# A decode step's last head pair: V between two parts of W_o, all its values as columns, W_o on whole partitions

## The chip, the cores and the metric

One core of a Trainium2 chip runs the kernel. The time is device time in microseconds (us) of one execution. A profiled execution also has a span, from its first to its last instruction, and the profile's times count from the span's start. TensorE does the matrix products, VectorE (DVE) and ScalarE (ACT) the element-wise work, GpSimd (POOL) some set-up, and SyncE (SP) issues nearly all the transfers from HBM, in one queue, over 16 DMA engines.

## The reference

Two sequences (B = 2) decode one token each. The first block is attention over a cache with 32 heads of 128, of 8192 positions each; the second a gated feed-forward block.

```
h  = x + A(layernorm(x))
h2 = h + F(layernorm(h))

A(x):  q = x @ wq                                  # 512 -> 32 heads x 128
       p = softmax(q . k_cache * 128**-0.5)        # per sequence and head, over 8192 positions
       return concat(p . v_cache) @ wo             # 4096 -> 512
F(x):  g = x @ W_gate;  u = x @ W_up               # 512 -> 1376
       return (max(g, 0) * u) @ W_down             # 1376 -> 512
```

All inputs are bfloat16. Each cache has 2 x 32 x 8192 x 128 elements, 134 MB; with the weights 281 MB have to come in from HBM.

## The kernel before

**Steps.** The 64 heads (32 of each sequence) are worked through in steps of four heads, 0 to 14 (14 is LASTQ, called Q); the last four heads are two pairs, p0 and p1. A step takes one tile of K and one of V, 8 MB each (4 MB for a pair): 128 partitions with 256 columns of 128 elements, so each partition holds 256 positions of one head (128 for a pair). Three buffers of this size, bufs[0] to bufs[2], go round. Everything is in an order written out by hand (manual_schedule), so that each engine and SP's queue take their instructions in program order.

**Scores.** products (L373) multiplies K by the broadcast q on VectorE, scores (L391, L393) sums each column's 128 elements by halving, in place. NPE columns of a step are done by TensorE instead (scores_pe: transposes, a copy on ScalarE per 8 columns, products with q). For p0 and p1, 40 columns are summed by ScalarE (act_sums, L379). The softmax takes the largest score: within a partition group for a four-head step (largest_of_own, no TensorE), through a product into PSUM for a pair (largest, L404), followed by exponentials on ScalarE (L431).

**Values.** values (L444) takes the shares of four columns as the stationary operand and 512 elements of V as the moving one, one product per four columns, into a PSUM row block; diagonals (L456) then picks the useful blocks out and turns them into columns. values_cols (L487) does the other way round: V's 128 x 128 block is stationary and two columns of shares move, and the result stands as a column at once. For p1 the kernel before does the first 64 of 128 columns by wide products (values_mixed, L468, then a copy on ScalarE and diagonals_mixed, L479) and the rest by values_cols into the same sums.

**Output projection.** W_o lies in the upper half of bufs[0]. The first 28 heads come in sets (SETS) with consecutive rows of W_o in one partition, so that a partition's piece is 16, 8 or 4 KB; the heads' results then have to be laid out anew to match (spread on VectorE, L499, lay_rows on TensorE and VectorE, L510 and L511), and attend_set (L517) multiplies. The last four heads are loaded by head, in rows of 1 KB, and attend (L524) takes them as they are:

```
for r0, r1 in ((0, P - 4), (P - 4, P)):            # L578: 124 rows, then 4
    nc.sync.dma_start(out=wo[r0:r1, HM * D:(HM + 2) * D]..., in_=_dram(A_wo, ...))
```

**The end.** hc (L640) adds the input. A normalisation and the feed-forward block follow: g_ps (gate), u_ps (up), d_ps (down, L690), whose weights are loaded last, gate and up into the upper half of bufs[2], W_down into bufs[1]. Only products with few columns are left there.

**Transfers.** A transfer's issue waits on SP until its buffer is free, and everything behind it in the queue waits as well. Each transfer signals one of eight semaphores in rotation, so an issue can also wait for the transfer eight places ahead of it. K of step i + 2 is issued when values of step i are done (it takes V's buffer), V of step i + 1 when scores of step i are done. The order at the end is: K of p0 and p1, V of p0, all of W_o (six transfers), V of p1 in four pieces (into the lower half of bufs[2], which values(Q) reads), gate, up in two parts, W_down in seven pieces.

Of the kernel before, what the change touches and what calls it, by code (L numbers as in the profile page):

```python
# [7 lines left out]
ACT = mybir.ActivationFunctionType  # L8
# [10 lines left out]
def _dram(t, offset, dims):  # L19
    return bass.AP(tensor=t.tensor, offset=t.offset + offset, ap=[list(d) for d in dims])  # L20
# [3 lines left out]
def kernel(  # L24
# [13 lines left out]
    nc = tc.nc  # L38
    P = nc.NUM_PARTITIONS
    B, Sq, D = A_x.shape  # L40
    _, Hkv, Sk, Dh = A_k_cache.shape
    Hq = A_wq.shape[1] // Dh
# [5 lines left out]
    f32 = mybir.dt.float32  # L48


    NH = 4
    NQ = Hq // NH
    LASTQ = B * NQ - 2
# [3 lines left out]
    VG = 4  # L57


    NPE = 32  # L60
    NPE_AT = {**{i: 24 for i in (1, 2)}, LASTQ: 24, LASTQ + 1: 0, LASTQ + 2: 0}
    NACT = 0
    NACT_AT = {LASTQ + 1: 40, LASTQ + 2: 40}
    NEXT = 16
    WIDE = 16
    QZ = 32


    SETS = [(0, 16, 0), (16, 8, 16), (24, 4, 24)]
    HM = 28  # L70
    SROWS = [n for _, n, _ in SETS]


# [87 lines left out]
    def load_tile(cache, s, dst, pieces=1):  # L161
        h = NH * s.g + (0 if s.quad else 2 * s.k)
        n = s.nt * Dh
        w = n // pieces
        for k in range(pieces):
            nc.sync.dma_start(
                out=dst[:, k * w:(k + 1) * w], in_=_dram(cache, (s.b * Hkv + h) * Sk * Dh + k * w, [[n, P], [1, w]]),
            )
# [19 lines left out]
    with tc.manual_schedule():  # L188
# [97 lines left out]
        o_ps = {}  # L286
# [96 lines left out]
        def scores(s):  # L383

            scol = scols[s.i]
            width = Dh
            while width > 8:
                half = width // 2
                lo = _free(s.kt, s.na * Dh, [[Dh, s.nv - s.na], [1, half]])
                hi = _free(s.kt, s.na * Dh + half, [[Dh, s.nv - s.na], [1, half]])  # L390
                nc.vector.tensor_tensor(out=lo, in0=lo, in1=hi, op=ALU.add)  # L391
                width = half
            nc.vector.tensor_reduce(  # L393
                out=scol[:, s.na:s.nv], in_=_free(s.kt, s.na * Dh, [[Dh, s.nv - s.na], [1, 8]]), axis=AXIS.X, op=ALU.add,
            )
            pms[s.i] = small.tile([P, 1], f32, tag="pm", name="pm", bufs=2)
            nc.vector.tensor_reduce(out=pms[s.i], in_=scol, axis=AXIS.X, op=ALU.max)  # L397
# [3 lines left out]
        def largest(s):  # L401

            mx[s.i] = ps.tile([P, P], f32, tag="mx", name="mx_ps")
            nc.tensor.matmul(out=mx[s.i], lhsT=_free(pms[s.i], 0, [[0, P]]), rhs=nscale, start=True, stop=True)  # L404
# [18 lines left out]
        def exponentials(s):  # L423
            scol = scols[s.i]
            nm = small.tile([P, NH], f32, tag="nm", bufs=2)
            nc.vector.tensor_reduce(
                out=nm[:, 0:s.nh], in_=mx[s.i].rearrange("p (j q) -> p j q", j=s.nh), axis=AXIS.X, op=ALU.min,
            )
            for j in range(s.nh):
                r = s.rows(j)  # L430
                nc.scalar.activation(  # L431
                    out=s.pg[r, :, j, :], in_=scol[r, :].rearrange("p (u t) -> p u t", t=VG), func=ACT.Exp, scale=SCALE,
                    bias=nm[r, j:j + 1], accum_out=s.zc[r, j:j + 1],
                )
# [24 lines left out]
                    start=(t == 0), stop=(t == VG - 1),  # L459
                )  # L460

        def values_mixed(s, u0, u1):

            r = slice(32 * (s.g % 4), 32 * (s.g % 4) + s.nh * VG)
            if u0 == 0:
                pv_ps[s.i] = ps2.tile([P, VG * Dh], f32, tag="o", name="pv_ps")
            for u in range(u0, u1):
                nc.tensor.matmul(  # L468
                    out=pv_ps[s.i][r, :], lhsT=s.pg[:, u].rearrange("p j t -> p (j t)"),
                    rhs=s.vt[:, u * VG * Dh:(u + 1) * VG * Dh], start=(u == 0), stop=(u == WIDE - 1),  # L470
                )
            if u1 == WIDE:
                nc.scalar.activation(out=pv[r, :], in_=pv_ps[s.i][r, :], func=ACT.Copy)

        def diagonals_mixed(s):
            h0 = NH * (s.g % 4)
            o_ps[s.i] = ps2.tile([P, 8], f32, tag="o", name="o_ps")
            for t in range(VG):
                nc.tensor.matmul(  # L479
                    out=o_ps[s.i][:, 0:2], lhsT=pv[:, t * Dh:(t + 1) * Dh],  # L480
                    rhs=pick[:, t].rearrange("p k j -> p (k j)")[:, h0:h0 + 2], start=(t == 0), stop=False,
                )

        def values_cols(s, t0, t1):

            for t in range(t0, t1):
                nc.tensor.matmul(  # L487
                    out=o_ps[s.i][:, 0:2], lhsT=s.vt[:, t * Dh:(t + 1) * Dh],
                    rhs=s.pg[:, t // VG, :, t % VG], start=False, stop=(t == s.nt - 1),
                )  # L490

        att_ps = ps.tile([P, KC, B], f32, tag="acc")
# [1 line left out]
        def spread(k, b):  # L494

            h0, n, _ = SETS[k]
            nq = Dh // n
            sp = qrep[:, B * k + b, :]
            nc.vector.tensor_tensor(  # L499
                out=_free(sp, 0, [[nq, n], [1, nq]]), in0=_free(ocol, h0 * B + b, [[B, n], [0, nq]]),  # L500
                in1=_free(quot[n], 0, [[0, n], [1, nq]]), op=ALU.mult,
            )
            return sp

        def lay_rows(k, sps):

            r = SROWS[k]
            or_ps = ps.tile([P, B, r], f32, tag="mx")
            for b in range(B):
                nc.tensor.matmul(out=or_ps[:, b, :], lhsT=sps[b], rhs=rest[r], start=True, stop=True)  # L510
            nc.vector.tensor_copy(orow[k], or_ps.rearrange("p b c -> p c b"))  # L511

        def attend_set(k, r0=0, r1=None):
            for c0 in range(r0, SROWS[k] if r1 is None else r1):
                for c in range(KC):
                    at = (SETS[k][2] + c0) * D + c * P
                    nc.tensor.matmul(  # L517
                        out=att_ps[:, c, :], lhsT=wo[:, at:at + P], rhs=orow[k][:, c0, :],
                        start=(k == 0 and c0 == 0 and c == 0), stop=False, skip_group_check=True,
                    )  # L520

        def attend(h):
            for c in range(KC):
                nc.tensor.matmul(  # L524
                    out=att_ps[:, c, :], lhsT=wo[:, h * D + c * P:h * D + (c + 1) * P], rhs=ocol[:, h, :],
                    start=False, stop=(h == Hq - 1), skip_group_check=True,
                )
# [43 lines left out]
        place_own(s)  # L571
        products(p0, 0, p0.na)
        own_sums(Q)
        for k, (h0, n, at) in enumerate(SETS):
            nc.sync.dma_start(
                out=wo[:, at * D:(at + n) * D], in_=_dram(A_wo, h0 * Dh * D, [[n * D, P], [1, n * D]]),
            )
        for r0, r1 in ((0, P - 4), (P - 4, P)):  # L578
            nc.sync.dma_start(
                out=wo[r0:r1, HM * D:(HM + 2) * D].rearrange("p (h n) -> p h n", n=D),  # L580
                in_=_dram(A_wo, (HM * Dh + r0) * D, [[D, r1 - r0], [Dh * D, 2], [1, D]]),
            )
        nc.sync.dma_start(
            out=wo[:, (HM + 2) * D:Hq * D].rearrange("p (h n) -> p h n", n=D),
            in_=_dram(A_wo, (HM + 2) * Dh * D, [[D, P], [Dh * D, 2], [1, D]]),
        )
        products(p0, p0.na)

        act_sums(p0)
        values(s, 0, s.nt // VG)  # L590
        load_tile(A_v_cache, p1, p1.vt, pieces=4)
        scores(p0)
        largest(p0)
        products(p1, 0, p1.na)
        exponentials(p0)
        act_sums(p1)
        products(p1, p1.na)
        for w, src, c, n in ((0, B_W_gate, 0, 4), (1, B_W_up, 0, 2), (1, B_W_up, 2, 2)):
            nc.sync.dma_start(
                out=wgu[:, w, c:c + n], in_=_dram(src, c * P * F, [[F, P], [P * F, n], [1, F]]),  # L600
            )
# [9 lines left out]
        nc.vector.reciprocal(out=rzs[Q], in_=z2_ps)  # L611
        values(p0, 0, p0.nt // VG)
        scores(p1)
        attend_set(0, 0, 10)
        diagonals(Q)
        largest(p1)
        attend_set(0, 10)
        normalise(Q)
        sps = [spread(1, b) for b in range(B)]
        exponentials(p1)  # L620
        lay_rows(1, sps)
        sps = [spread(2, b) for b in range(B)]
        attend_set(1)
        lay_rows(2, sps)
        values_mixed(p1, 0, WIDE)
        attend_set(2)
        diagonals_mixed(p1)
        values_cols(p1, VG * WIDE, 3 * p1.nt // 4)
        for h in range(HM, HM + 2):
            attend(h)  # L630
        sums(Q + 2)
        shares(Q + 2)
        values_cols(p1, 3 * p1.nt // 4, p1.nt)
        normalise(Q + 2)
        for h in range(HM + 2, Hq):
            attend(h)


# [93 lines left out]
```

## Time and profile before

| | |
|---|---|
| time, median of 3 runs | 665.35 us (664.29 to 665.5) |
| the profiled execution: its own time, its span | 664.98 us, 663.2 us |
| busy: PE, PEld, DVE, ACT | 54%, 24%, 83%, 20% of the span |
| from HBM | 281.09 MB, 424 GB/s over the span |
| mean granted TensorE clock | 0.773 |
| V of p1: issued, four pieces of 1 MB | 630.08 us and later; 14.0 us to landing (median) |
| W_o, first 16 heads | issued 605.50 us, 25.0 us to landing |
| hc starts; span ends | 654.52 us; 663.2 us |

PE is the matrix products and PEld the loads of their stationary operand. Lnnn is a line of the kernel. Rows of the timeline and of the chain of waits begin with a start and a length in us. The chain follows the work that ended last back through what released it. The windows give, for a stretch of time, the busy time of each engine with its number of instructions in brackets, the granted TensorE clock, the busy share of the DMA engines and the GB/s that they moved.

### The profile page before, as it was taken

How to read it: one execution, taken by the hardware profiler on the slowest of the kernel's cores; microseconds unless marked ns; L12 is line 12 of the kernel's file. 1: busy time of each engine (PE TensorE's matmuls, PEld its weight loads, DVE VectorE, ACT ScalarE, POOL GpSimd, SP SyncE). 2: the span in 40 equal slices, each digit the busy share in tenths (PEclk: the TensorE clock that was granted, in tenths of full speed). 3: DMA queues.
4: the chain of work that ended last, by engine and by line, in shares of the span. 5: the costliest groups of instructions: out<-in, count | busy, mean ns of one | idle time of the engine just before them, and what ended most of it. 6: DMA issues, size and time to landing. Idle time of an engine off the chain costs nothing.

```text
span 663.2 us, 5113 instructions
## 1 busy us (share of the span) xinstructions
PE 357.5 (54%) x2105; PEld 161.1 (24%) x2105; DVE 551.1 (83%) x245; ACT 131.6 (20%) x372; POOL 5.3 (1%) x32
## 2 busy tenths in 40 slices
PE   3530924719184572918358191835719277273787
PEld 1210311304032230403114040311304133021345
DVE  1399697979969797996969799696988979999971
ACT  1130030301103030210303011030300205102760
POOL 3000000000000000000000000000000000000000
PEclk9875876959688695968769596876959779595986
DMA  9999999999999999999999999999999999999995
GB/s 380 443 440 443 443 424 411 435 439 432 443 436 435 415 440 431 432 439 439 432 427 439 428 423 443 432 443 427 432 431 428 435 435 432 427 422 431 417 366 226
DMA packets 8562, 281.40 MB, mean 424 GB/s; under 512 B 858, under 2 KB 2012, under 8 KB 3420
## 3 DMA queue, kind: packets, MB, share of 16 engines
q1 hardware_dynamic: 8536, 281.09, 98.7%
q8 instruction: 16, 0.26, 0.2%
q14 instruction: 6, 0.05, 0.0%
q10 hardware_dynamic: 4, 0.00, 0.0%
HBM read 281.09 MB, written 0.00 MB: 424 GB/s over the span
## 4 chain that ended last, share of the span: by engine, by line
DVE 44%; DMA 33%; PE 19%; ACT 3%; issue 1%; DVEq 0%; ACTq 0%
DMA tile<-in_A_k_cache_dram 31%; DVE tile L373 20%; DVE tile L391 19%; PE pv_ps L444 14%; DVE scol L393 2%; DMA tile<-in_A_wq_dram 2%; ACT tile L379 2%; PE q_ps L253 1%; PE pv_ps L468 1%; DVE pgq L418 1%; ACT ecol L413 1%; DVE pm L397 1%; DVE qrep L393 0%; DVE pm L408 0%; PE o_ps L487 0%
## 5 line engine op out<-in xcount | busy, mean ns | idle before, releaser
L444 PE MATMUL pv_ps<-tile,pgq 128*16 128x512 bf16 x960 | 238.9, 416 | 199.5 <-DVE pgq L418 187.1
L373 DVE TENSOR_TENSOR tile<-tile,qrep 128x28672 bf16<-128x28672 bf16 (+3 forms) x16 | 228.1, 14258 | 55.5 <-DMA tile<-in_A_k_cache_dram 55.5
L391 DVE TENSOR_TENSOR tile<-tile 128x14336 bf16<-128x14336 bf16 (+5 forms) x68 | 233.2, 3429 | 2.3
L444 PEld LDWEIGHTS <-pgq 128*16 128x16 bf16 x960 | 91.6, 97 | 341.2 <-DVE pgq L418 197.4
L350 ACT ACTIVATE tile<-t_ps 128x1024 bf16<-128x1024 bf16 x57 | 56.7, 1022 | 18.4 <-PE t_ps L349 17.5
L449 ACT ACTIVATE pv<-pv_ps 16x512 f32<-16x512 f32 (+1 forms) x16 | 9.4, 588 | 243.3 <-PE pv_ps L444 243.3
L340 PE MATMUL row_ps<-tile,qz 128*32 128x512 bf16 (+1 forms) x114 | 34.8, 387 | 18.6 <-ACT tile L350 18.3
L413 ACT ACTIVATE ecol<-scol,nmax 128x256 bf16<-128x256 f32 x14 | 7.1, 507 | 188.1 <-DVE nmax L412 188.1
L349 PE MATMUL t_ps<-ident,tile 128*128 128x128 bf16 x456 | 34.0, 225 | 5.4 <-DMA tile<-in_A_k_cache_dram 5.4
L349 PEld LDWEIGHTS <-tile 128*128 128x128 bf16 x456 | 26.9, 101 | 22.2 <-issue 16.6
L393 DVE TENSOR_REDUCE scol<-tile 128x224 f32<-128x1792 bf16 (+1 forms) x14 | 28.4, 2029 | 0.5
L308 PE MATMUL z_ps<-zc,ones 128*128 128x16 f32 (+1 forms) x8 | 2.4, 373 | 43.6 <-DVE zc L299 43.6
L379 ACT ACTIVATE tile<-tile 128x128 bf16<-128x128 bf16 x80 | 23.4, 294 | 3.5 <-DVE tile L373 3.5
L418 DVE TENSOR_TENSOR pgq<-ecol,ownb 128x1024 bf16<-128x1024 bf16 x15 | 10.4, 692 | 10.3 <-ACT ecol L413 10.3
L373 DVE TENSOR_TENSOR tile<-tile,qpair 128x5120 bf16<-128x5120 bf16 (+1 forms) x4 | 17.7, 4416 | 0.0
L340 PEld LDWEIGHTS <-qz 128*32 128x32 bf16 (+1 forms) x114 | 9.4, 94 | 28.7 <-issue 22.4
L379 ACT ACTIVATION_READ_ACCUMULATOR tile<-tile 128x1 f32 x80 | 15.0, 187 | 0.0
L256 DVE CAST tile<-q_ps 2x512 bf16<-2x512 f32 x8 | 5.4, 679 | 10.3 <-PE q_ps L253 10.3
L253 PE MATMUL q_ps<-tile,xn 128*2 128x512 bf16 x32 | 9.3, 452 | 8.6 <-DMA tile<-in_A_wq_dram 8.6
L365 ACT ACTIVATE scol<-sc_ps 32x32 f32<-32x32 f32 (+1 forms) x56 | 12.2, 217 | 7.8 <-PE sc_ps L360 7.3
L308 PEld LDWEIGHTS z_ps<-zc,ones 128*128 128x128 f32 x8 | 2.0, 312 | 43.9 <-DVE zc L299 29.0
L360 PE MATMUL sc_ps<-ident_f,tile 32*128 32x32 f32 (+1 forms) x60 | 6.5, 226 | 11.0 <-ACT tile L357 11.0
(127 smaller groups left out, 132.6 us busy)
## 6 DMA issues: line engine op xcount, KB each, us to landing
tile<-in_A_k_cache_dram SPq DMA_DIRECT2D x2, 4096.0 KB, 23.2
tile<-in_A_wq_dram SPq DMA_DIRECT2D x1, 4096.0 KB, 12.3
tile<-in_A_v_cache_dram SPq DMA_DIRECT2D x1, 4096.0 KB, 20.5
tile<-in_A_v_cache_dram SPq DMA_DIRECT2D x4, 1024.0 KB, 14.0
tile<-in_A_wo_dram SPq DMA_DIRECT2D x1, 2048.0 KB, 25.0
tile<-in_B_W_gate_dram SPq DMA_DIRECT2D x1, 1376.0 KB, 16.8
tile<-in_B_W_up_dram SPq DMA_DIRECT2D x2, 688.0 KB
tile<-in_A_wo_dram SPq DMA_DIRECT2D x1, 1024.0 KB, 27.4
```

What stands on the lines that cost most here:

```text
L253: nc.tensor.matmul(out=q_ps, lhsT=xn[:, c, :], rhs=wq_sb[:, c, n0:n0 + 4 * Dh], start=(c == 0), stop=(c == KC - 1),)
L340: nc.tensor.matmul(out=row_ps, lhsT=z, rhs=s.kt[:, (nv + c0 + k) * Dh:(nv + c0 + k + 4) * Dh], start=(u == 0), stop=(u == U - 1),)
L349: nc.tensor.transpose(t_ps[:, k, :], s.kt[:, t * Dh:(t + 1) * Dh], ident)
L350: nc.scalar.activation(out=s.kt[:, (nv + c0) * Dh:(nv + c0 + TPC) * Dh], in_=t_ps.rearrange("p t s -> p (t s)"), func=ACT.Copy,)
L365: nc.scalar.activation(out=scols[s.i][r, nv:s.nt].rearrange("p (u t) -> p t u", t=4), in_=sc_ps[r, :, :, j], func=ACT.Copy,)
L373: nc.vector.tensor_tensor(out=kv, in0=kv, in1=_free(s.qr, 0, [[0, n], [1, Dh]]), op=ALU.mult)
L379: nc.scalar.activation(out=kv, in_=kv, func=ACT.Copy, accum_out=scols[s.i][:, t:t + 1])
L391: nc.vector.tensor_tensor(out=lo, in0=lo, in1=hi, op=ALU.add)
L393: nc.vector.tensor_reduce(out=scol[:, s.na:s.nv], in_=_free(s.kt, s.na * Dh, [[Dh, s.nv - s.na], [1, 8]]), axis=AXIS.X, op=ALU.add,)
L413: nc.scalar.activation(out=ecol, in_=scols[s.i], func=ACT.Exp, scale=SCALE, bias=nmax, accum_out=zs[:, s.b, s.g:s.g + 1],)
L418: nc.vector.tensor_tensor(out=s.pg, in0=_free(ecol, 0, [[VG, s.nt // VG], [0, NH], [1, VG]]), in1=_free(ownb, 0, [[0, s.nt // VG], [VG, NH ...
L444: nc.tensor.matmul(out=pv_ps[s.i][r, :], lhsT=s.pg[:, u].rearrange("p j t -> p (j t)"), rhs=s.vt[:, u * VG * Dh:(u + 1) * VG * Dh], start= ...
```

## The change

Steps 3 to 6 give 24 columns to TensorE instead of 32, as steps 1 and 2 did already. W_o is cut into sets of 16, 8, 4 and 2 heads and one piece with the last two, each on all 128 partitions. On SP's queue V of the last pair comes after the first set, and the rest of W_o after V. The gate is loaded in two parts. All 128 columns of the last pair's V are taken by values_cols; values_mixed and diagonals_mixed are gone. On TensorE the first set is attended whole ahead of the last pair's maximum, the maximum is ahead of diagonals(Q), and the other sets and the last heads are attended after all values are done.

```diff
-    NPE_AT = {**{i: 24 for i in (1, 2)}, LASTQ: 24, LASTQ + 1: 0, LASTQ + 2: 0}
+    NPE_AT = {**{i: 24 for i in range(1, 7)}, LASTQ: 24, LASTQ + 1: 0, LASTQ + 2: 0}
-    WIDE = 16
-    SETS = [(0, 16, 0), (16, 8, 16), (24, 4, 24)]
-    HM = 28
+    SETS = [(0, 16, 0), (16, 8, 16), (24, 4, 24), (28, 2, 28)]
+    HM = 30
...
-        def values_mixed(s, u0, u1):
...
-        def diagonals_mixed(s):
...
         def values_cols(s, t0, t1):
+            if t0 == 0:
+                o_ps[s.i] = ps2.tile([P, 8], f32, tag="o", name="o_ps")
             for t in range(t0, t1):
                 nc.tensor.matmul(
                     out=o_ps[s.i][:, 0:2], lhsT=s.vt[:, t * Dh:(t + 1) * Dh],
-                    rhs=s.pg[:, t // VG, :, t % VG], start=False, stop=(t == s.nt - 1),
+                    rhs=s.pg[:, t // VG, :, t % VG], start=(t == 0), stop=(t == s.nt - 1),
                 )
...
-        for k, (h0, n, at) in enumerate(SETS):
+        def load_set(k):
+            h0, n, at = SETS[k]
             nc.sync.dma_start(
                 out=wo[:, at * D:(at + n) * D], in_=_dram(A_wo, h0 * Dh * D, [[n * D, P], [1, n * D]]),
             )
-        for r0, r1 in ((0, P - 4), (P - 4, P)):
-            nc.sync.dma_start(
-                out=wo[r0:r1, HM * D:(HM + 2) * D].rearrange("p (h n) -> p h n", n=D),
-                in_=_dram(A_wo, (HM * Dh + r0) * D, [[D, r1 - r0], [Dh * D, 2], [1, D]]),
-            )
-        nc.sync.dma_start(
-            out=wo[:, (HM + 2) * D:Hq * D].rearrange("p (h n) -> p h n", n=D),
-            in_=_dram(A_wo, (HM + 2) * Dh * D, [[D, P], [Dh * D, 2], [1, D]]),
-        )
+        load_set(0)
         products(p0, p0.na)
 
         act_sums(p0)
         values(s, 0, s.nt // VG)
         load_tile(A_v_cache, p1, p1.vt, pieces=4)
+        for k in range(1, len(SETS)):
+            load_set(k)
+        nc.sync.dma_start(
+            out=wo[:, HM * D:Hq * D].rearrange("p (h n) -> p h n", n=D),
+            in_=_dram(A_wo, HM * Dh * D, [[D, P], [Dh * D, Hq - HM], [1, D]]),
+        )
...
-        for w, src, c, n in ((0, B_W_gate, 0, 4), (1, B_W_up, 0, 2), (1, B_W_up, 2, 2)):
+        for w, src, c, n in ((0, B_W_gate, 0, 2), (0, B_W_gate, 2, 2), (1, B_W_up, 0, 2), (1, B_W_up, 2, 2)):
...
         values(p0, 0, p0.nt // VG)
         scores(p1)
-        attend_set(0, 0, 10)
+        attend_set(0)
+        largest(p1)
         diagonals(Q)
-        largest(p1)
-        attend_set(0, 10)
+        exponentials(p1)
         normalise(Q)
-        sps = [spread(1, b) for b in range(B)]
-        exponentials(p1)
-        lay_rows(1, sps)
-        sps = [spread(2, b) for b in range(B)]
-        attend_set(1)
-        lay_rows(2, sps)
-        values_mixed(p1, 0, WIDE)
-        attend_set(2)
-        diagonals_mixed(p1)
-        values_cols(p1, VG * WIDE, 3 * p1.nt // 4)
-        for h in range(HM, HM + 2):
-            attend(h)
+        sps = [[spread(k, b) for b in range(B)] for k in range(1, len(SETS))]
+        half = p1.nt // 2
+        values_cols(p1, 0, half)
+        for k in range(1, len(SETS)):
+            lay_rows(k, sps[k - 1])
         sums(Q + 2)
         shares(Q + 2)
-        values_cols(p1, 3 * p1.nt // 4, p1.nt)
+        values_cols(p1, half, p1.nt)
         normalise(Q + 2)
-        for h in range(HM + 2, Hq):
+        for k in range(1, len(SETS)):
+            attend_set(k)
+        for h in range(HM, Hq):
             attend(h)
```

More of the change, by code (lines that the diff above doesn't have):

```diff
@@ L460, in diagonals @@
                 )
-        def values_mixed(s, u0, u1):
[L464 to L470, printed above, removed]
-                )
-            if u1 == WIDE:
-                nc.scalar.activation(out=pv[r, :], in_=pv_ps[s.i][r, :], func=ACT.Copy)
-        def diagonals_mixed(s):
[L476 to L481, printed above, removed]
-                )
         def values_cols(s, t0, t1):
+            if t0 == 0:
+                o_ps[s.i] = ps2.tile([P, 8], f32, tag="o", name="o_ps")
             for t in range(t0, t1):
@@ L577 @@
             )
-        for r0, r1 in ((0, P - 4), (P - 4, P)):
-            nc.sync.dma_start(
-                out=wo[r0:r1, HM * D:(HM + 2) * D].rearrange("p (h n) -> p h n", n=D),
-                in_=_dram(A_wo, (HM * Dh + r0) * D, [[D, r1 - r0], [Dh * D, 2], [1, D]]),
-            )
-        nc.sync.dma_start(
-            out=wo[:, (HM + 2) * D:Hq * D].rearrange("p (h n) -> p h n", n=D),
-            in_=_dram(A_wo, (HM + 2) * Dh * D, [[D, P], [Dh * D, 2], [1, D]]),
-        )
+        load_set(0)
         products(p0, p0.na)
```

## The prediction

> **What bounds the kernel now.** I read the page first for who is busy: the transfers. Section 2 has the core's DMA engines at nine tenths in every slice but the last, while the bytes per second fall only in the last two slices.
>
> ```profile
> DMA  9999999999999999999999999999999999999995
> GB/s 380 443 440 443 443 424 411 435 439 432 443 436 435 415 440 431 432 439 439 432 427 439 428 423 443 432 443 427 432 431 428 435 435 432 427 422 431 417 366 226
> ```
>
> The trace's record of completions (one per DMA engine and transfer) says it more sharply: on the engine that finishes first, each 8 MB tile lands 19.35 us after the one before it, for all 30 tiles in the steps. Nothing that computes costs time there as long as each load is issued before the one ahead of it has drained. The end of the span is different, so I then read the chain of waits from its end (start, length, what):
>
> ```profile
> 639.82 0.60 ACT pv L449
> 640.46 1.06 PE o_ps L456 x8
> 641.52 0.32 PE mx_ps L404 x2
> ...
> 643.90 5.89 PE pv_ps L468 x16
> 649.82 0.04 issue
> 649.87 0.60 ACT pv L473
> 650.47 0.04 issue
> 650.51 1.05 PE o_ps L479 x8
> 651.57 0.82 PE o_ps L487 x32
> ```
>
> From about 640 us TensorE's order of work sets the end, and its largest piece is the last pair's 16 wide products (L468, 5.89 us). The same 32 column products that follow take 0.82 us. Last, the windows of 2 us around the transfers of W_o (columns: busy times, granted clock, DMA share, GB/s):
>
> ```profile
> 630.00:632.00 2.00, 2.00 (x7) 0.66 (x6) 2.00 (x1) 2.00 (x15) 0.00 (x0) 0.62 1.01 371
> 632.00:634.00 2.00, 2.00 (x11) 0.80 (x10) 2.00 (x3) 2.00 (x15) 0.00 (x0) 1.00 1.02 287
> 634.00:636.00 2.00, 2.00 (x11) 0.78 (x9) 1.97 (x2) 2.00 (x15) 0.00 (x0) 1.00 1.08 287
> 636.00:638.00 2.00, 2.00 (x45) 1.28 (x43) 1.97 (x2) 2.00 (x15) 0.00 (x0) 1.00 0.99 313
> 638.00:640.00 2.00, 0.14 (x6) 0.05 (x3) 1.93 (x3) 1.98 (x14) 0.00 (x0) 1.00 1.06 436
> ```
>
> The engines are fully busy, yet move 287 GB/s instead of some 425. This is when W_o's 1 KB rows (L579, L583) pass; by the packet records they take 66 ns each, and 8 KB packets beside them over 400 ns instead of 312. The 124-row piece completes on four engines only (634.9, 635.6, 637.5 and 638.1 us). Two of the four were among the latest already. The lag between first and last engine was 3.5 us when the first 16 heads landed (627.0 to 630.5) and is 5.1 us when the last quarter of V does (643.5 to 648.65). The last piece of W_down lands at 659.09, on the lagging engine; its first use would be at about 660.2. So behind TensorE's chain the transfers are only 1 us away from being the bound.
>
> **Part 1, steps 3 to 6 with 24 columns by TensorE instead of 32.** VectorE gets 8 columns more. The chain shows both sizes: the product is 15.63 us with 232 columns and 15.10 with 224, the four additions 7.90, 4.03, 2.10, 1.14 against 7.63, 3.90, 2.04, 1.10, the sum 2.10 against 2.03; together 1.1 us a step. TensorE and ScalarE lose 8 transposes, two wide products and a 1.02 us copy (L350). V's next load is issued when the scores are done; in these steps that is 4.35 us before the first engine drains, and becomes 3.2. K's load, behind the values, has 4.1 to 5.6 and becomes 3.0 or more. The smallest margin in the trace, at the V load of step 13, is 2.3 us, and no engine went dry there. Cost: nothing. The cover is that margin; without it each of four steps would pay up to 1.1 us.
>
> **Part 2, the order on SP's queue.** V of the last pair goes behind the first 16 heads of W_o. Its four issues wait for values(Q) in quarters (32 of the 64 products from 607.68 us, so until about 617), and SP holds the rest of W_o, the gate, up and down loads behind them. At 617 us V of the first pair (lands at 625.6) and 2 MB of W_o are still queued, and the first engine runs dry at 627.0, so the wait is hidden with some 10 us of cover. Later issues wait for a completion eight transfers back; in the new order each finds at least 4 us of work queued. Before, the last two W_down pieces went out only at 652.2 and 653.9, after gate and the first half of up. Now the gate comes in two parts and they wait for its second part and the first half of up, due near 649 and 651.
>
> W_o's pieces become 8, 4 and 2 KB rows and one piece of 1 KB rows (256 packets instead of 512), all on 16 engines. On the lagging engine, with measured differences between successive landings: 630.5 + four quarters of V at 2.5 + the 1 MB and 0.5 MB sets at 2.47 and 1.26 + 8 packets of 2 KB at 0.65 (between 46 ns for 1 KB and 111 ns for 2.75 KB) + 16 of 1 KB at 0.8 to 1.1 + gate 3.46 + up 3.44 + down 0.33 + 1.88 + four at 0.34 = 656.3 us. To it comes what I can't see: the slowdown beside the 1 KB rows, nothing to 1.2 us (half of the 2.1 to 2.6 us that the windows above lost), and an instruction fetch of 1 us that may hit this engine or not. I take 0.6 in all, since the 1 KB pieces of W_down at the end run at 46 to 49 ns and slow nobody: 656.9 us, 2.2 earlier than now. Bounds 656.3 and 658.5.
>
> **Part 3, TensorE's chain.** The first set's 64 products are done by 638.9 (40 took 1.15 us from 636.99), inside the wait for the maximum, which VectorE delivers at 640.40. Taken ahead of the diagonals, the largest (0.49 us) is done at 640.9 instead of 641.85; the exponentials follow the reduction on VectorE and four ScalarE pieces (642.05 to 643.42 now), so the shares stand at 642.3 us. The diagonals (1.06) fit in between; behind them queue normalise and six spreads (VectorE, 0.48 a pair), done near 643.7, under the columns. Columns: 64 at 0.87 us for 32 is 1.74, to 644.1; their V landed by 635.5, where before the second quarter came at 643.63 and was itself what the wide products waited for. Three lay_rows at 0.40 each (two products 0.14, copy 0.18, two handovers): 645.3. Sums 0.43, columns 1.74, normalise 0.2: 647.7. Then 64 products of attend that used to lie partly under other work, 0.99 for 32: 649.7. hc starts at about 649.7 instead of 654.52, 4.8 us earlier. What goes is 5.89 + 0.60 + 1.05 with three handovers; what comes is 1.74 of columns, one lay_rows and the attends.
>
> That rests on the row of 0.82 to 0.99 us for 32 column products with their weight loads (0.98 us for 32), at half as at full granted clock. [...]
>
> **The sum.** hc to the end takes 8.7 us now (654.52 to 663.2), so the chain alone would end at 658.4. But gate lands near 650, up near 653.5, and W_down at 656.9, on which d_ps then waits: four products and the handover 0.25, and from y to the end 2.85 (660.35 to 663.2): 660.0 us, 3.2 less than now. The transfers take the bound from TensorE and keep 1.6 of its 4.8 us. The profiled execution took 664.98 us for its span of 663.2, so 661.8; against the median of 665.35, which is 0.4 higher, 662.2.
>
> **The rivals.**
>
> *The lag stays.* If the slow windows come from reading W_o's rows at all, the last piece still lands at 659.1 and the end is 659.1 + 3.1 = 662.2, 1.0 us gained: 664.3. For it: half of the 1 KB packets are still there. Against: the lag grew on just those engines that took the 124 rows. Chance 0.10.
>
> *TensorE's chain stays the bound.* If I overrate the down loads, 658.4 to 659, gain 4.2 to 4.8: 660.8. It needs the lagging engine to speed up to 655.5, below the sum with no penalty. Chance 0.06.
>
> *Slower: the loads of steps 3 to 6 run dry.* VectorE's 1.1 us is paid four times as soon as a load needs more than 3.2 us from issue to first byte: 4.4 us lost against 3.2 gained, 1.2 slower, 666.5. Against: the margin of 2.3 us at step 13 without a gap. For: VectorE is the busiest engine (83%), idle only 3.5 us before each product. Chance 0.07, with everything else that ends slower.
>
> [...] Chance 0.05.
>
> **How the numbers follow.** The forecast has the remaining 0.72, between 661.4 (656.3 as the last landing) and 663.7 (658.5), of which none is within 0.2% of the median. That share, 1.3 us, is about what a measurement of this kernel can tell; the three runs shown differ by 1.2. The range takes in the chain as the bound and the lag that stays, 660.9 to 664.4. Faster: 0.72 + 0.06 and some of the lag, 0.81. Within 0.2%: most of the lag and of the chain not freed, 0.11. Slower: 0.08.
>
> **What would show it.** Right: in the chain of waits, L468 and L479 gone, hc at about 650, and d_ps waiting for W_down; windows from 630 us at 400 GB/s or more; V's quarters issued before 620 us; first-engine landings still 19.35 us apart in steps 3 to 6. Wrong: a DMA share under 0.9 between 130 and 310 us, an idle TensorE ahead of the columns for V, or d_ps starting with no wait.

## The result, and the profile after

The changed kernel takes 661.55 us in the median of six runs (661.18 to 662.02), the kernel before 665.25 in six (664.29 to 666.09): ratio 0.9945, 95% interval [0.9932, 0.9958], 3.7 us faster. The forecast was 662.2. The profiled execution took 661.18 us with a span of 659.4, against a forecast span of 660.0.

The two rows of the page for the 40 slices of the span, as they stood before the prediction:

```profile
DMA  9999999999999999999999999999999999999997
GB/s 382 445 442 445 402 430 437 445 446 434 402 441 434 441 438 417 437 429 438 441 430 425 433 426 441 441 422 441 418 442 434 430 433 433 430 421 430 423 410 273
```

Nothing dips in the slices of steps 3 to 6, and the last two slices hold 410 and 273 GB/s where they held 366 and 226. The windows where W_o passes (the same columns as before):

```profile
630.00:632.00 2.00, 2.00 (x7) 0.54 (x5) 2.00 (x1) 2.00 (x15) 0.00 (x0) 0.50 1.01 422
632.00:634.00 2.00, 2.00 (x6) 0.61 (x5) 2.00 (x3) 2.00 (x15) 0.00 (x0) 0.50 1.00 418
634.00:636.00 2.00, 2.00 (x9) 0.75 (x8) 1.98 (x1) 2.00 (x15) 0.00 (x0) 0.86 1.04 434
636.00:638.00 2.00, 2.00 (x11) 0.78 (x9) 1.95 (x2) 2.00 (x16) 0.00 (x0) 1.00 0.99 414
638.00:640.00 2.00, 2.00 (x62) 1.56 (x61) 1.93 (x3) 1.98 (x14) 0.00 (x0) 1.00 1.01 418
```

The stretch of 287 GB/s is gone. The end of the chain of waits:

```profile
638.03 12.80 DMA tile<-in_B_W_up_dram
650.83 0.02 issue
650.85 0.02 SPq L583
650.86 0.03 issue
650.89 5.32 DMA tile<-in_B_W_down_dram
656.21 0.05 issue
656.26 0.28 PE d_ps L664 x4
656.54 0.02 issue
656.56 0.18 DVE y L669
```

Before, this view ran from 640 us through TensorE's products and copies. Now it runs through two transfers: the last piece of W_down lands at 656.21 us (before 659.09), and d_ps (L664) has only four products left to do. TensorE's timeline shows what stands where the wide products were (start, length, what; in brackets the idle time before and what ended it):

```profile
640.49 0.49 PE L403 MATMUL mx_ps<-nscale,pm 128*128 128x128 f32 x2 [0.21 <-DVE pm L396]
640.82 1.21 PE L455 MATMUL o_ps<-pick,pv 128*128 128x14 f32 x8
642.45 1.85 PE L466 MATMUL o_ps<-pgp,tile 128*128 128x2 bf16 x64 [0.42 <-ACT pgp L430]
...
650.82 1.25 PE L634 MATMUL g_ps<-hn,tile 128*128 128x2 bf16 x41 [0.46 <-DVE hn L621]
652.60 0.22 PE L634 MATMUL g_ps<-hn,tile 128*128 128x2 bf16 x3 [0.52 <-issue]
...
654.69 1.83 PE L664 MATMUL d_ps<-hm,tile 128*128 128x2 bf16 x44 [0.26 <-DVE hm L659]
```

The maximum (L403) comes first, 64 column products (L466) take 1.85 us and wait for the exponentials, not for V. The last row is the new wait: d_ps takes 1.83 us for 44 products where 1.32 is its length without a wait. The row of L634 above it is a gap that I had not foreseen, 0.52 us in which TensorE waits for nothing that the profile shows. The row of hc on VectorE, 4.97 us earlier than before:

```profile
649.55 0.17 DVE L614 TENSOR_TENSOR hc<-att_ps,xres 128x8 f32<-128x8 f32 x1 [1.54 <-PE att_ps L503]
```

### The profile page after: what moved, and what is told of

It is laid out like the page before. It is cut to its first block, busy times and chain, and to the rows that moved or that the text cites. A ratio compares the mean times of both kernels' runs of the same rounds, so it can differ in the third digit from the quotient of the medians.

```text
span 659.4 us, 5114 instructions
## 1 busy us (share of the span) xinstructions
PE 349.5 (53%) x2107; PEld 157.9 (24%) x2107; DVE 556.6 (84%) x250; ACT 126.6 (19%) x367; POOL 5.3 (1%) x32
## 4 chain that ended last, share of the span: by engine, by line
DVE 44%; DMA 36%; PE 18%; ACT 1%; issue 1%; DVEq 0%; ACTq 0%; SPq 0%
DMA tile<-in_A_k_cache_dram 31%; DVE tile L372 20%; DVE tile L390 19%; PE pv_ps L443 16%; DVE scol L392 2%; DMA tile<-in_B_W_up_dram 2%; DMA tile<-in_A_wq_dram 2%; PE q_ps L252 1%; DMA tile<-in_B_W_down_dram 1%; DVE pgq L417 1%; ACT ecol L412 1%; DVE pm L396 1%; DVE qrep L392 0%; DVE pm L407 0%; DVE hmax L409 0%
## 5 line engine op out<-in xcount | busy, mean ns | idle before, releaser
L349 ACT ACTIVATE tile<-t_ps 128x1024 bf16<-128x1024 bf16 x53 | 52.6, 1022 | 18.1 <-PE t_ps L348 17.5
L339 PE MATMUL row_ps<-tile,qz 128*32 128x512 bf16 (+1 forms) x106 | 32.4, 387 | 18.8 <-ACT tile L349 18.7
L348 PE MATMUL t_ps<-ident,tile 128*128 128x128 bf16 x424 | 31.5, 225 | 5.5 <-DMA tile<-in_A_k_cache_dram 5.5
L348 PEld LDWEIGHTS <-tile 128*128 128x128 bf16 x424 | 25.1, 101 | 20.6 <-issue 14.9
```

Source lines behind the costliest of these rows:

```text
L339: nc.tensor.matmul(out=row_ps, lhsT=z, rhs=s.kt[:, (nv + c0 + k) * Dh:(nv + c0 + k + 4) * Dh], start=(u == 0), stop=(u == U - 1),)
L348: nc.tensor.transpose(t_ps[:, k, :], s.kt[:, t * Dh:(t + 1) * Dh], ident)
L349: nc.scalar.activation(out=s.kt[:, (nv + c0) * Dh:(nv + c0 + TPC) * Dh], in_=t_ps.rearrange("p t s -> p (t s)"), func=ACT.Copy,)
```

## The experiments

The theory: two chains end side by side, TensorE's (from hc on) and the transfers' (from the last landing on), and the later one sets the end. The change shortens both, the first by the columns and the early maximum, the second by loading W_o on whole partitions; the 24 columns and the place of V's loads are worth nothing by themselves. The rivals were that one part does it all, that slow transfers come from 1 KB rows or from the four engines, and that the 24 columns or V's place matter. All experiments but e2 are edits of the changed kernel, and each was timed beside the kernel before, in 5 to 12 executions (the medians of the kernel before: 664.6 to 665.24 us).

Two lengths turn a trace into an expected span. From the last landing to the end it is 3.19 us (656.21 to 659.4). From hc to the end, without a wait for W_down, it is 8.7 us before; after, d_ps could have started at 654.69 and taken 1.32, 0.53 less than it took, so the chain alone would have ended at 658.9, 9.35 after hc (the gap is in it). The table sets the later of the two against the span.

| run | median us | ratio [95%] | hc | last landing | chain's end | transfers' end | span |
|---|---|---|---|---|---|---|---|
| after | 661.55 | 0.9945 [0.9932, 0.9958] | 649.55 | 656.21 | 658.9 | **659.4** | 659.4 |
| e1 chain only | 663.87 | 0.9982 [0.9974, 0.9991] | 651.16 | 658.84 | 660.5 | **662.0** | 662.0 |
| e2 transfers only | 665.65 | 1.0007 [0.9998, 1.0017] | 654.57 | 657.07 | **663.3** | 660.3 | 663.2 |
| e3 32 columns again | 661.46 | 0.9949 [0.9937, 0.9961] | 649.76 | 656.16 | 659.1 | 659.4 | 659.8 |
| e4 124 + 4 rows | 663.65 | 0.9976 [0.9968, 0.9985] | 649.99 | 658.57 | 659.3 | **661.8** | 661.9 |
| e10 64 + 64 rows of 1 KB | 663.12 | 0.9967 [0.9954, 0.9980] | 649.96 | 658.09 | 659.3 | **661.3** | 661.4 |
| e12 64 + 64 rows of 8 KB | 667.04 | 1.0021 [1.0010, 1.0032] | 650.38 | 661.24 | 659.7 | **664.4** | 664.5 |
| e5 maximum after diagonals | 662.72 | 0.9962 [0.9950, 0.9974] | 651.46 | 656.19 | **660.8** | 659.4 | 660.9 |
| e6 V behind all of W_o | 661.40 | 0.9948 [0.9936, 0.9960] | 649.28 | 656.25 | 658.6 | **659.4** | 659.4 |
| e7 16 columns, steps 3 to 10 | 663.06 | 0.9976 [0.9966, 0.9986] | 651.11 | 657.56 | 660.5 | **660.8** | 660.7 |
| e8 8 columns, steps 3 to 10 | 666.65 | 1.0028 [1.0016, 1.0040] | 654.28 | 661.07 | 663.6 | **664.3** | 664.3 |

(e2's chain is the one before, so its length is 8.7.) One row is off by more than 0.1 us: in e3 the unforeseen gap, 0.49 us there, fell into d_ps behind the last landing, and its span is 0.4 us longer than the later of the two ends.

### e1 and e2: each half alone

e1 keeps the changed order on TensorE with the transfers and the sets of the kernel before; e2 is the kernel before, wide products included, with the changed transfers and the one more lay_rows that the fourth set needs. Both give TensorE 32 columns in steps 3 to 6.

```diff
 # e1, against the changed kernel
-    SETS = [(0, 16, 0), (16, 8, 16), (24, 4, 24), (28, 2, 28)]
-    HM = 30
+    SETS = [(0, 16, 0), (16, 8, 16), (24, 4, 24)]
+    HM = 28
...
+        for r0, r1 in ((0, P - 4), (P - 4, P)):
...
 # e2, against the kernel before
-    SETS = [(0, 16, 0), (16, 8, 16), (24, 4, 24)]
-    HM = 28
+    SETS = [(0, 16, 0), (16, 8, 16), (24, 4, 24), (28, 2, 28)]
+    HM = 30
...
+        load_set(0)
...
         load_tile(A_v_cache, p1, p1.vt, pieces=4)
+        for k in range(1, len(SETS)):
+            load_set(k)
...
```

> The new chain on TensorE (all 128 columns, maximum ahead of diagonals, attends last) over the old transfers (three sets, 124 and 4 rows, all of W_o ahead of V, gate in one part, old steps 3 to 6). If the transfers' last landing on the lagging engine bounds the end (theory): it stays at 659.1 us and the span ends 3.1 to 3.2 later, 662.2 to 662.3, 1.0 us less than before. If the shorter chain alone made the gain (rival): 659.4, 3.8 less. If column products are no cheaper than wide ones: 663.2, no gain.

> The new transfers (four sets and the last two heads on 128 partitions, V of the last pair after the first set, gate in two parts) under the old chain (64 columns by wide products, diagonals ahead of the maximum, old steps 3 to 6). Theory: the last landing moves to about 656.3 us, but TensorE's chain still ends where it did, so the span changes by -0.4 (V is there earlier) to +0.4 (one more lay_rows). Rival, the transfers alone made the gain: 3 to 4 us less.

In e1 both kinds of wait return on TensorE's timeline, for V ahead of the last 32 columns and for W_down in d_ps:

```profile
648.40 1.01 PE L466 MATMUL o_ps<-pgp,tile 128*128 128x2 bf16 x32 [1.49 <-DMA tile<-in_A_v_cache_dram]
657.55 1.60 PE L668 MATMUL d_ps<-hm,tile 128*128 128x2 bf16 x28 [0.46 <-DMA tile<-in_B_W_down_dram]
```

The chain of waits in e2 ends on TensorE, with the wide products in it and d_ps in one piece:

```profile
644.97 4.95 PE pv_ps L468 x16
...
650.81 0.91 PE o_ps L479 x8
...
654.57 0.18 DVE hc L641
...
659.06 1.32 PE d_ps L691 x44
```

The chain alone brings 1.4 us (665.24 − 663.87), the transfers alone nothing that can be told from zero, both together 3.7. Neither is the whole gain, and some 2.3 us of it exist only when both are there: this is what two bounds of nearly equal length look like. e4 below, which puts back the divided rows of W_o alone, loses 2.1 us.

e2's last landing is 0.86 us later than in the changed kernel with the same transfers. The delay begins at the 1 MB set of W_o, which lands on the last engine 3.32 us after the transfer ahead of it (2.48 in the changed kernel). Just there an instruction packet of 16 KB runs, 1.03 us from 641.75 us. The trace doesn't say which engine carried it, so that it is the cause is likely and not shown.

### e4, e10 and e12: what makes W_o's transfers slow

e4 splits the one piece with 1 KB rows as before, 124 and 4 rows. e10 splits it into 64 and 64, where each half runs on all 16 engines. e12 leaves that piece whole and splits the set of eight heads, whose rows are 8 KB, into 64 and 64.

```diff
 # e4; e10 has ((0, P // 2), (P // 2, P)), and e12 this split around the load of SETS[1]
+        for r0, r1 in ((0, P - 4), (P - 4, P)):
-            out=wo[:, HM * D:Hq * D]..., [[D, P], [Dh * D, Hq - HM], [1, D]]
+            out=wo[r0:r1, HM * D:Hq * D]..., [[D, r1 - r0], [Dh * D, Hq - HM], [1, D]]
```

> The changed kernel with its one piece of two heads in 1 KB rows split into 124 and 4 rows. Theory: four engines take 62 and 2 packets of 1 KB instead of 16, at 50 to 70 ns 2.4 to 3.4 us more on them; at least one of them is a lagging engine, so the last landing moves from 656.2 to 658.0 or later and the span grows by 1.8 to 3.4 us; the windows show 290 GB/s for some us. Rival, the loss came from W_o's 1 KB rows as such or from their place ahead of V: no change beyond 0.3 us.

> [...] Theory, few engines with many packets are the cost: no loss beyond 0.3 us, windows at 390 GB/s or more. [...]

> The changed kernel with W_o's second set (8 heads, rows of 8 KB, 1 MB) split into 64 and 64 rows; everything else on 128 partitions. If the slow windows come from engines that take other partitions than in the transfers next to it, the size of a row doesn't matter: some 290 GB/s while this set passes, 2 us or more lost (the set is twice as many bytes as the 1 KB piece). If only 1 KB rows suffer: 400 GB/s or more and no loss beyond 0.3 us.

The windows of 2 us of e4, and behind them those of e10 and of e12, where the divided rows pass (last column GB/s, before it the DMA share):

```profile
642.00:644.00 2.00, 2.00 (x47) 1.97 (x47) 1.02 (x6) 0.83 (x4) 0.00 (x0) 0.50 1.01 315
644.00:646.00 2.00, 1.23 (x35) 1.01 (x32) 0.87 (x5) 0.00 (x0) 0.00 (x0) 0.50 1.05 274
646.00:648.00 2.00, 2.00 (x63) 2.00 (x63) 0.17 (x1) 0.00 (x0) 0.00 (x0) 0.50 1.04 306
```

```profile
642.00:644.00 2.00, 1.33 (x45) 1.25 (x45) 1.38 (x7) 0.80 (x4) 0.00 (x0) 0.59 1.01 295
644.00:646.00 2.00, 1.23 (x34) 1.02 (x31) 0.50 (x3) 0.00 (x0) 0.00 (x0) 0.50 1.04 283
646.00:648.00 2.00, 2.00 (x64) 2.00 (x65) 0.17 (x1) 0.00 (x0) 0.00 (x0) 0.50 1.04 310
```

```profile
638.00:640.00 2.00, 1.83 (x65) 1.67 (x64) 1.93 (x3) 1.98 (x15) 0.00 (x0) 1.00 0.95 221
640.00:642.00 2.00, 1.49 (x7) 1.49 (x8) 0.64 (x3) 0.73 (x2) 0.00 (x0) 0.61 1.02 221
642.00:644.00 2.00, 2.00 (x50) 1.97 (x51) 1.14 (x7) 0.71 (x4) 0.00 (x0) 0.50 1.00 228
644.00:646.00 2.00, 1.22 (x31) 1.01 (x28) 0.75 (x5) 0.00 (x0) 0.00 (x0) 0.50 1.04 227
```

All three show engines that are busy and slow. In e4 the slow stretch of before is back with one edit and costs 2.1 us in the median (663.65 against 661.55); its 124-row part completes on four engines (645.9, 646.6, 647.7 and 648.2 us). I had put the cause there. e10 uses no four-engine transfer and is nearly as slow, 1.6 us in the median and 2.0 in the span (e4: 2.5): four engines are not needed for it. e12 has no small rows in the divided set and loses most, 5.5 us in the median, 5.1 in the span: rows of 1 KB are not needed either. What the three share is a transfer that does not cover all 128 partitions. They also have one transfer more, but the engines don't sit idle for it: the DMA share stays at 0.95 or more. The changed kernel moves 387 to 411 GB/s from 642 to 648 us, where its undivided 1 KB rows pass:

```profile
642.00:644.00 2.00, 1.57 (x60) 1.55 (x58) 1.38 (x7) 0.40 (x2) 0.00 (x0) 0.50 1.03 387
644.00:646.00 2.00, 1.23 (x22) 1.02 (x19) 0.50 (x3) 0.00 (x0) 0.00 (x0) 0.50 1.04 395
646.00:648.00 2.00, 2.00 (x78) 2.00 (x79) 0.33 (x2) 0.00 (x0) 0.00 (x0) 0.50 1.05 411
```

e12 also shows that its neighbours pay. The divided set is 1 MB; at 221 instead of 430 GB/s that is 4.7 us for 2.4, a loss of 2.3. The windows stay at half rate for 8 us, and the last landing is 5.0 us late. Its 8 KB packets take 549 to 596 ns in that stretch (means of 2 us), where they take about 312 elsewhere.

Why these shapes are slow isn't shown: the runs show only which ones are, and no record says which partitions an engine writes.

### e5: the maximum after the diagonals

```diff
-        largest(p1)
         diagonals(Q)
+        largest(p1)
```

> The changed kernel with the last pair's maximum behind diagonals(Q) again. TensorE's chain gets 1.1 us longer: hc at 650.6 instead of 649.55 us. Theory, the transfers bound the end and the chain has slack: the span grows by 0 to 0.5 us, since d_ps would start near 655.5 and still has to wait for the last landing at 656.2. Rival, the chain still sets the end: 1.1 us more.

A miss: the median is 1.2 us above the changed kernel's (the two intervals just overlap), the span 1.5. TensorE's timeline of e5:

```profile
640.38 1.89 PE L455 MATMUL o_ps<-pick,pv 128*128 128x14 f32 x8 [1.66 <-ACT pv L448]
642.11 0.78 PE L403 MATMUL mx_ps<-nscale,pm 128*128 128x128 f32 x2
644.36 1.85 PE L466 MATMUL o_ps<-pgp,tile 128*128 128x2 bf16 x64 [1.47 <-DMA tile<-in_B_W_gate_dram]
```

I had taken 1.06 us for the diagonals, from the trace of before, where the granted clock was 1.00 from 639 to 641 us. In e5 it was 0.50 from 640 on, and the eight fp32 products take 1.89 us, the maximum behind them 0.78 instead of 0.49. The columns start at 644.36, 1.91 later than in the changed kernel, and hc is as much later. (The row names a transfer of the gate as releaser of the columns, which they do not read; the exponentials end at 644.3 on ScalarE, and those they need.) The fall of the clock is not e5's own: in e3, which has the changed order, it is 0.55 from 640 to 641 us and the diagonals take 1.73 us, yet hc is only 0.2 us later than in the changed kernel. With the maximum ahead, the diagonals lie beside the exponentials even so (in e3 they end at 642.72 us, the exponentials at 642.61); with it behind, they are paid. The second thing that e5 shows is the slack: 1.91 us of a longer chain became 1.5 of span, so the changed chain had 0.4 to 0.5 to give. The end of e5's chain of waits has no wait for W_down, and the unforeseen gap is in it:

```profile
653.99 0.62 issue
...
656.70 1.32 PE d_ps L664 x44
```

### e6: V behind all of W_o

```diff
-        load_set(0)
-        products(p0, p0.na)
...
+        for k in range(len(SETS)):
             load_set(k)
```

> The changed kernel with all of W_o (on 128 partitions) ahead of the last pair's V on SP's queue, as before. The same bytes, so the same last landing, 656.2 us. V's four quarters land 5 us later (638 to 645.5), which the columns (from 642.4 and from 646.0) need last at 645.96. Theory: no difference beyond 0.3 us, the place of V is free. Rival, the place of V is what pays: 1 us or more lost.

661.40 us: the place of V makes no difference. Its quarters land at up to 645.67 us instead of 640.5, in time for the columns that read them, and the last landing is the same.

### e3, e7 and e8: columns given to TensorE in the steps

```diff
-    NPE_AT = {**{i: 24 for i in range(1, 7)}, LASTQ: 24, LASTQ + 1: 0, LASTQ + 2: 0}
+    NPE_AT = {**{i: 24 for i in (1, 2)}, LASTQ: 24, LASTQ + 1: 0, LASTQ + 2: 0}   # e3
+    NPE_AT = {**{i: 24 for i in (1, 2)}, **{i: 16 for i in range(3, 11)}, ...}     # e7; e8 has 8 for 16
```

> The changed kernel with steps 3 to 6 back at 32 columns by TensorE. Theory: no difference to the changed kernel beyond 0.3 us, the V loads of these steps are issued 1.1 us earlier (4.4 us ahead of the first engine's last byte instead of 3.3). Rival, the steps give or cost something (less load on TensorE and ScalarE, another granted clock): 1 us or more either way.

> The changed kernel with 16 columns by TensorE in steps 3 to 10 (24 in steps 3 to 6 and 32 after, in the changed kernel). VectorE has 2.3 us more in a step than with 32, so V's loads are issued 2.1 to 2.2 us ahead of the first engine's last byte instead of 3.3 to 4.4. Theory, any margin above the smallest seen so far (2.3, no gap) or close to it is free: no difference beyond 0.3 us. Rival, the margin of 3.3 was nearly used up: 1.1 us a step, up to 9 us lost.

> The changed kernel with 8 columns by TensorE in steps 3 to 10. V's loads are issued only 1.0 us ahead of the first engine's last byte, and VectorE, which idles 3.5 us a step with 32 columns, has 3.4 us more work. Theory: this is where the margin runs out; if a load needs 1.0 to 1.5 us from issue to its first byte, the first engines go dry by up to 0.5 us a step and the successive first landings show more than 19.36 us, 0 to 4 us lost in eight steps. If VectorE becomes the bound as well, more than that. Rival, no loss: then the margin doesn't matter at all down to 1 us.

32 or 24 columns are the same (661.46 and 661.55), as forecast. At 16 over eight steps I expected nothing and got 1.5 us in the median. V's loads then have 1.9 to 2.8 us between their issue and the moment when the first engine drains, all but one at most 2.35, and the landings on that engine, 19.35 us apart before and after, come up to 19.89 apart; by the end it is 2.3 us late, the last engine 1.35, since part of the loss falls into the lag between the two. At 8 columns the margins are 1.1 to 2.3, the distances up to 20.18, and the span is 4.9 us longer.

The packet records show where this time goes. A row of K or V, 64 KB, takes 2.42 us. From 160 to 560 us 12 such rows take over 0.05 us longer in the changed kernel, 66 in e7 and 154 in e8, and in e7 and e8 most of these lie where one load follows another; per engine that is 0.4, 1.9 and 3.4 us. Engines without any packet add 0.0, 0.2 and 1.3 us. Away from the handovers a row takes 2.42 to 2.43 us on average in all three, so VectorE's greater load doesn't slow the transfers as such.

The limit isn't sharp. In e7 and e8 a load with 2.4 us of margin or more lost at most 0.1 us on the first engine, and one with less lost between nothing and 0.8 (one of 1.93 us lost nothing, one of 2.27 lost 0.54). The changed kernel's smallest margin in these steps, 3.3, is about 1 us away from it.

### e9 and e11: trying to gain more

Both bounds lie within 0.5 us of one another, so a faster version has to shorten both. e9 loads V in two pieces instead of four and W_down in five instead of seven; e11 also lays each set's rows between the columns.

```diff
-    FSETS = [(0, 3), (3 * P, 3), (6 * P, 1), (7 * P, 1), (8 * P, 1), (9 * P, 1), (F - P, 1)]
+    FSETS = [(0, 3), (3 * P, 3), (6 * P, 3), (9 * P, 1), (F - P, 1)]
-        load_tile(A_v_cache, p1, p1.vt, pieces=4)
+        load_tile(A_v_cache, p1, p1.vt, pieces=2)
 # e11
-        half = p1.nt // 2
-        values_cols(p1, 0, half)
         for k in range(1, len(SETS)):
+            values_cols(p1, 32 * (k - 1), 32 * k)
             lay_rows(k, sps[k - 1])
+        values_cols(p1, 96, 112)
```

> The changed kernel with the last pair's V in two pieces (16 KB rows at 614 ns instead of two of 8 KB at 313) and nine of W_down's eleven row groups in three pieces of 3 KB rows (124 ns instead of three times 46). Per engine 16 x 12 ns and 8 x 14 ns less, 0.3 us: last landing 655.9 instead of 656.2, span 0.0 to 0.4 us shorter, since TensorE's chain in the changed kernel ends only 0.5 us before the transfers do.

> The same with the three lay_rows each behind 32 columns, so that the waits for their copies (three times 0.26 us) lie under columns. TensorE's chain is 0.8 us shorter; the transfers stay the bound: span 0.2 to 0.6 us shorter than the changed kernel's, and no better than the version with fewer packets alone by more than 0.3 us.

Neither can be told from the changed kernel: 661.41 us, 0.9945 [0.9933, 0.9958], and 661.28 us, 0.9944 [0.9930, 0.9958]. e9's last piece lands at 656.14, only 0.07 earlier, and d_ps has 16 products behind its last wait instead of 4. In e11 hc starts at 648.30, 1.25 us earlier than in the changed kernel, which brings nothing, since the transfers (last landing 655.95, 0.26 earlier) set the end.

The part that the transfers gained is lost again at the very end. The output lands at 658.50 us in e9 and at 658.31 in e11 (658.57 in the changed kernel), but from there the span lasts 1.08 us instead of 0.83. SP closes the kernel with five instructions that wait for the transfers' semaphores, always in the same order and some 0.06 us apart. In the changed kernel the output's transfer signals a semaphore of the fifth, and the other four are done before it lands (657.78 to 658.00). With four transfers fewer the rotation gives it one of the first, and all the others, 0.25 us, come behind the landing. In e4, e10 and e12, with one transfer more, it is one of the third; from the output's landing to the end it is 0.93 us there, the 0.1 us by which their spans in the table exceed the transfers' end.

## Why the prediction was right

**The bound.** As forecast, the transfers took it over from TensorE, and d_ps waits for W_down. e1 and e2 show that both halves were needed, and in the table the later of the two ends is the span, but for e3, where the gap lies behind the last landing.

**The transfers' sum.** 656.3 us from measured differences, 656.21 measured. Up to the sets of W_o it holds step by step: the last quarter of V lands at 640.5 on the last engine (630.5 + 4 × 2.5), the sets at 642.94 and 644.23 (642.97 and 644.23 by the sum). Behind them small errors cancel: the 1 KB rows took 0.71 us instead of 0.8 to 1.1, gate and up (landed at 649.10 and 652.62) 3.52 each instead of 3.46 and 3.44.

The term that was mis-sized is the 0.6 us added for the slowdown beside the 1 KB rows and an instruction fetch (a 16 KB packet of the page's kind instruction): in the profiled execution it measured 0. For the slowdown that has a reason: the divided rows were gone with the change, and on all 128 partitions the 256 packets of 1 KB took 49 ns each, where 512 had taken 66 before, in windows of 2 us with 387 GB/s or more. For the instruction packets it looks like luck. They ran at 642.97, 650.04 and 653.97 us, some 1.1 us each, and the last engine's landings didn't move; in e2 and e8 such a landing came 0.8 and 0.9 us late just where a packet ran (641.75 and 651.27 us).

Without the 0.6 the forecast is 661.6 (the prediction writes 661.4 for a last landing at 656.3, but its own sum gives 661.6). That this is the median found is partly chance as well: three of the six executions took 661.18 to 661.26 us and three 661.84 to 662.02, and the only trace is from the first group. What the other three lost isn't known.

**The cause of the slow windows.** The rival on the lag stood on the reading of W_o at all; against it I put the engines that took the 124 rows. The rival is wrong: the last piece lands at 656.21 us and not at 659.1, and when the last part of up lands, the lag is 3.4 us (649.25 to 652.62), where before it was 5.1 (650.44 to 655.54). My reason was only partly right: it was the divided rows, but neither the four engines (e10) nor the 1 KB rows (e12) were needed.

**TensorE's chain.** hc at 649.7 was forecast and 649.55 measured; 64 columns at 1.74, measured 1.85, 29 ns a product with its weight load. The slack behind the chain was mis-sized: I had it end at 658.4, 1.6 us ahead of the transfers, and it would have ended at 658.9, 0.5 ahead. The difference is the gap of 0.52 us in g_ps, which the row of 8.7 us before did not have, and the transfers' 0.6. So e5, which I expected to be nearly free, was not.

**Steps 3 to 6 and SP's queue.** Both at no cost, as forecast (e3, e6). V's loads have 3.3 to 3.4 us of margin where 3.2 was forecast, K's 3.6 to 4.8 where 3.0 or more was, and V of the last pair was issued from 611.07 to 616.58 us, ahead of the forecast 617. The cover named there, a margin of 2.3 us without a loss, lies about where loads begin to cost (e7 and e8), but it was one reading: the same load, V's of step 13, had 2.6 us in the changed kernel and 1.1 to 1.7 in e1 to e5 and e12, where its landing on the first engine came 0.1 to 0.5 us late.

**The rival on the slower side** (loads run dry) is refuted for 24 columns, but its mechanism begins one size further on: e7 loses 1.5 us, and e8 is slower than the kernel before. The price was less than the rival's 1.1 us a step: 1.3 us of span for the eight steps of e7.

## What to carry to other kernels

Where two bounds end within a microsecond or two of each other, cost both to their ends and take the later: each half of the change alone gave 1.4 us and nothing, both 3.7. When bytes per second fall while the DMA engines stay busy, look at the partitions that the transfers cover before looking at row sizes or counts of engines: here divided rows passed at 221 to 315 GB/s, undivided ones at 387 or more. And a sum of measured differences between landings was right to 0.1 us over 26 us, with some help from errors that cancelled; in the addition for what could not be seen, one half was charged without a cause and the other was left to luck.

## What the runs showed of the hardware that I had not expected

- While the transfers over 124 or 64 partitions passed (e4, e10, e12), the core moved 221 to 315 GB/s at a DMA share of 0.95 or more, and what was in flight beside them was slowed too: 1 MB in two halves of 64 partitions cost 5.1 us of span.
- TensorE has a gap of 0.40 to 0.62 us that waits for nothing the profile shows. In the changed kernel, e5, e6, e9 and e10 it stands before the same product, the third from the end of g_ps. Counted over the trace's records of TensorE, with its weight loads and its sequencer's instructions, that product is number 4033 in the changed kernel; in e3, which has 80 records more, the gap stands before number 4289, and in e7, which has 240 fewer, before 3777: each 256 away, at another product. The 16 KB instruction packet ahead of each gap had ended 0.7 to 1.2 us before it, and no run was aimed at the gap: the cause is open.
- The same eight fp32 products took 1.06 us at a granted clock of 1.00 and 1.73 to 1.89 at 0.50 to 0.55 (e3, e5), while 64 bf16 products with two columns took 1.75 us at 1.00 (the first set's, from 638.53 in the changed kernel) and 1.85 at 0.50 (the columns from 642.45). What may run at a low clock has to be priced by kind.
- The kernel's last waits cost by their order: the same output transfer was followed by 0.83, 0.93 or 1.08 us to the end of the span, after which of SP's five last waits its semaphore belongs to.
- A load of 8 MB that was issued less than about 2.4 us before the one ahead of it drained lost up to 0.5 us at 16 columns and up to 0.8 at 8, mostly as longer packets at the handover and less as idle engines; with more margin it lost at most 0.1.
